# FNet and GeGLU on one core: row moments of h taken by ScalarE, places for gate/up weights four tiles ahead, and the last low half of the hidden DFT weights on VectorE

## The chip, the core and the metric

The kernel runs on one core of one Trainium2 chip. The core has five engines with a queue each: TensorE (PE: matmuls, with weight loads shown as PEld), VectorE (DVE), ScalarE (ACT), GpSimd (POOL) and SyncE (SP), which here issues every DMA transfer. Each engine takes its own instructions in the order in which they were written, and waits for others by semaphores. All DMA goes through one queue of SyncE onto 16 DMA engines. The metric is the device time of one execution in microseconds (us).

## The reference

A pre-LayerNorm FNet mixing layer, followed by a GeGLU feed-forward layer, in float32. S = 2048 tokens, D = 448, DF = 1792.

```python
def _layernorm(x, axis=-1, eps=1e-5):
    m = jnp.mean(x, axis=axis, keepdims=True)
    v = jnp.var(x, axis=axis, keepdims=True)
    return (x - m) / jnp.sqrt(v + eps)
...
a = jnp.einsum("bsd,ed->bse", x, dft_hid_re)
b = jnp.einsum("bsd,ed->bse", x, dft_hid_im)
y = jnp.einsum("ts,bse->bte", dft_seq_re, a) - jnp.einsum("ts,bse->bte", dft_seq_im, b)
...
g = jnp.einsum("bsd,df->bsf", x, w_gate)
u = jnp.einsum("bsd,df->bsf", x, w_up)
h = _gelu(g) * u
return jnp.einsum("bsf,fd->bsd", h, w_down)
...
x = A_x
h = x + _A_ref(_layernorm(x, axis=-1), A_dft_seq_re, A_dft_seq_im, A_dft_hid_re, A_dft_hid_im)
h2 = h + _B_ref(_layernorm(h, axis=-1), B_w_gate, B_w_up, B_w_down)
```

## The kernel before

Every float32 operand of a matmul is split into two float16 parts: ScalarE writes the high half (`hi_part`, line 100) and VectorE the low half (`lo_part`, lines 104 and 106), and a product takes three matmuls. Some products are formed by Strassen's scheme of seven, whose operand sums VectorE or GpSimd form first. All engines' instructions stand in the order in which the program writes them; a table of slots (`slots`, `plan`, with a rank inside a slot) sets that order for the middle of the kernel, and a loop over tiles for its end.

**First tiles (0 to 40 us).** x comes in 16 tiles of 128 tokens. VectorE takes the mean and variance of a row (`x_stats`, BATCH_NORM), ScalarE the root, VectorE the reciprocal with one Newton step (`rstd`, lines 128 to 132) and the normalised tile (line 137). Its halves `xs` are transposed by TensorE for tiles 0 to 3 (`x_turn_pe`, line 374) and by DMA after that, and `feature_mm` (line 412) multiplies them by the hidden DFT weights, which come as four slabs `wh_raw` and are split into `wh_hi` and `wh_lo`. The low half of slab 3 (64 rows) is written by GpSimd in two operations (`wh_low(3, G)`, lines 399 and 400), those of the other slabs by VectorE in one (line 106).

**Sequence DFT (to 362 us).** Eight passes `p` of eight units `u`; each unit loads a block `wr` of DFT weights, splits it into `ws` and runs 48 or 84 matmuls into `acc` (line 508). A place of `wr` is loaded again when its low half has been taken. Into the same slots are woven: the gate/up weights (`Weights`: 14 tiles of 128 columns are loaded as `gu_raw`, summed to `gu_s`, split to `gu_w` and stored as `w_dram`); `seq_out(p)`, in which VectorE adds the bank sums of a pass, over a scratch tile `e`, to x and so makes h in `hx`; and one slot after it the moments of h for the second LayerNorm, `ffn_moments` on VectorE (lines 175 and 176), the root on ScalarE (line 121), `rstd` and, for the first four passes, the normalised operand for the gate/up stage (`xn_h` by ScalarE, its sums and halves, and its transposes by DMA into `hops`). Pass `p` is token pair `(q, j)` with p = 2q + j. The last pair's moments, (3, 1), are taken later, in the tile loop.

**Gate/up and down (362 us to the end).** 56 tiles, `t` = 14 q + f: a quarter `q` of the tokens, against a slab `f` of 128 gate and 128 up columns. `GateUp` does a tile's products into three banks pX, pY and pZ (line 913); in the first quarter a tile is 39 matmuls. The weights of a tile, `gw[t]`, are 0.9 MB read back from `w_dram` (`gw_load`, line 996) into one of three places: two of the pool `ring` and one of `ring3`. Tiles 0, 1 and 2 lie there already, from the split. In iteration t the load of tile t + 2 is issued, and it waits in SyncE's queue until TensorE has last read tile t - 1. The hidden values go into `hh[q]`, two places of a pool `fpool`; `hh[1]` is first written in tile 14. Beside the first quarter the down weights are prepared (`down_prep`): seven loads (line 190), sums by GpSimd (lines 195 to 198), halves by ScalarE and VectorE. From tile 14 on the down products (line 855) run between the gate/up products.

```python
def gw_load(t):
    gw[t] = w_tile(f"gw{t}", ring if t % 3 < 2 else ring3)
    nc.sync.dma_start(gw[t], w_dram[t % NF])
...
if 0 < t < N_GU - 2:
    gw_load(t + 2)
```

Of the kernel before, what the change touches and what calls it, by code (L numbers as in the profile page):

```python
# [32 lines left out]
def kernel(  # L33
# [84 lines left out]
    def root(mv, tag):  # L118
        n = mv.shape[1]
        sd = small.tile([P, n], F32, tag=f"sd{n}", name=f"sd_{tag}")  # L120
        A.activation(sd, mv[:, :, 1], AF.Sqrt, scale=1.0 / X_SC**2, bias=eps_t)
        return sd

    def rstd(mv, sd, tag, pool=small):
# [4 lines left out]
        V.tensor_scalar(r[:, 1], mv[:, :, 1], EPS, -0.5 / X_SC**2, op0=ALU.add, op1=ALU.mult)  # L129
# [40 lines left out]
    def ffn_moments(q, j, h, g):  # L170
# [4 lines left out]
        V.bn_stats(st, h[:, g, :])  # L175
        V.bn_aggr(moments[q, j][:, g, :], st)

    def ffn_root(q, j):
        moments[q, j] = moments[q, j], root(moments[q, j], f"h{q}_{j}")

    def ffn_rstd(q, j):
        mv, sd = moments[q, j]
        moments[q, j] = mv, rstd(mv, sd, f"h{q}_{j}", const)
# [16 lines left out]
    def ffn_norm(q, j, h):  # L200
        tag = f"h{q}_{j}"
        mv, r = moments.pop((q, j))
        xn = fops.tile([P, 2, D], F32, tag="xn", name=f"xn_{tag}")
        for g in range(2):
            normed(xn[:, g, :], h[:, g, :], mv, r, g)
        ffn[q, j] = xn

    def ffn_norm_act(q, j, h):
# [4 lines left out]
        nb = small.tile([P, 2], F32, tag="nb", name=f"nb_{tag}")  # L213
        V.scalar_tensor_tensor(nb, mv[:, :, 0], -1.0, r, op0=ALU.mult, op1=ALU.mult)
# [91 lines left out]

    def x_stats(*tiles):
        n, tag = len(tiles), f"x{tiles[0]}"
        mv = small.tile([P, n, 2], F32, tag=f"mv{n}", name=f"mv_{tag}")
# [4 lines left out]
        norm_x[tiles] = mv  # L314
# [10 lines left out]
    def x_bias(*tiles):  # L325
        mv, r, _ = norm_x[tiles[0]]
        nb = small.tile([P, 2], F32, tag="nb", name=f"nb_x{tiles[0]}")
        V.scalar_tensor_tensor(nb, mv[:, :, 0], -1.0, r, op0=ALU.mult, op1=ALU.mult)
# [7 lines left out]
    def x_norm_v(i):  # L336
# [6 lines left out]
        u, g = divmod(i, 2)  # L343
        if g == 0:
            pool = (fops, p1)[ORDER.index(u) % 2]
            t = pool.tile([P, 2, 2 * D], F16, tag="xs", name=f"xs{u}")
            for k in range(2):
                xs[i + k] = t[:, k, :]
# [179 lines left out]

    def seq_out(p):
        (X, Y, Z, W), _ = acc.pop(p)  # L530
        h = hp[divmod(p, 2)]
        e = fops.tile([P, 4, HD], F32, tag="tt", name=f"e{p}")
# [144 lines left out]
    for p in range(N_PASS):  # L677
# [11 lines left out]
        for g in range(2):  # L689
            plan(n + 1, 5, lambda q=q, j=j, g=g: ffn_moments(q, j, hp[q, j], g))  # L690
# [45 lines left out]
    wh_low(3, G)  # L736
# [15 lines left out]
    x_norm(3)  # L752
    x_lo(3)
# [239 lines left out]

    def gw_load(t):
        gw[t] = w_tile(f"gw{t}", ring if t % 3 < 2 else ring3)
# [173 lines left out]

    cur = GateUp(0)  # L1170
# [6 lines left out]
    for t in range(N_GU):  # L1177
# [5 lines left out]
        if 0 < t < N_GU - 2:  # L1183
            gw_load(t + 2)
# [126 lines left out]
```

## Time and profile before

| | us |
|---|---|
| median of 3 runs (lowest to highest) | 728.72 (728.53 to 728.88) |
| the profiled execution's own time | 728.71 |
| its span, first to last instruction | 726.9 |
| TensorE busy, share of the span | 712.0, 98% |
| mean granted TensorE clock | 0.998 |

How to read the rows below. A row of a timeline has the start (us from the span's first instruction), the time from the first start to the last end, the engine, the line, the operation, what it writes and reads (buffer numbers left out), the shape, how many equal instructions were merged, and in brackets the idle time ahead and what ended it. A row of windows has a stretch, its length, each engine's busy time with its count of instructions (PE, PEld, DVE, ACT, POOL), the granted TensorE clock as a share of full speed (PEclk), the share of the 16 DMA engines that was busy, and GB/s. SPq is SyncE's queue; it issues transfers and is not counted as busy. Where a time is called drawn, it is the matmul's modelled end.

The page's coarse view, 40 equal slices of the span with the busy share of each engine in tenths:

```profile
PE   7999999999999999999999999999999999999998
DVE  6678859998989888989345567576665756667520
ACT  5476644645555545444155555456555545555510
POOL 3023030000000000020014464465563756657230
DMA  8274444897969699685067754757458486555401
```

VectorE is nearly full from slice 7 to slice 18 (110 to 340 us), GpSimd does almost nothing there, and ScalarE stands at about half throughout.

### The profile page before, as it was taken

The page shows a single profiled execution, that of the slowest core. Times are in us where ns is not written, and L with a number is a line of the kernel's source. Part 1 is how long each engine was busy: PE and PEld are TensorE (multiplying, and loading weights), DVE is VectorE, ACT ScalarE, POOL GpSimd, SP SyncE. Part 2 cuts the span into 40 slices and gives each one's busy share as a digit, 9 for nine tenths or more (in the row PEclk, how much of TensorE's full clock was granted, in tenths as well). Part 3 has the DMA queues.
Part 4 walks back from the last instruction along what each step waited for, and adds up shares of the span by engine and source line. Part 5 has one row for each costly group of instructions (what it writes and reads, how often), then busy time and mean ns, then how long its engine had stood idle before and what let it go on. Part 6 is the DMA issues. An engine that isn't in the chain of part 4 may idle for free.

```text
span 726.9 us, 14535 instructions
## 1 busy us (share of the span) xinstructions
PE 712.0 (98%) x5800; PEld 561.6 (77%) x5800; DVE 510.6 (70%) x1043; ACT 365.0 (50%) x748; POOL 207.9 (29%) x237
## 2 busy tenths in 40 slices
PE   7999999999999999999999999999999999999998
PEld 5556566666767666676788789999999999999998
DVE  6678859998989888989345567576665756667520
ACT  5476644645555545444155555456555545555510
POOL 3023030000000000020014464465563756657230
PEclk9999999999999999999999999999999999999999
DMA  8274444897969699685067754757458486555401
GB/s 326 60 187 93 73 171 148 287 256 259 276 240 282 234 275 326 242 298 187 1 223 240 243 191 169 198 179 223 163 171 205 162 215 223 204 200 203 153 15 64
DMA packets 72340, 142.90 MB, mean 197 GB/s; under 512 B 41296, under 2 KB 47568, under 8 KB 72272
## 3 DMA queue, kind: packets, MB, share of 16 engines
q1 hardware_dynamic: 72272, 141.97, 61.1%
q8 instruction: 45, 0.74, 0.4%
q14 instruction: 23, 0.19, 0.1%
HBM read 112.46 MB, written 20.19 MB: 182 GB/s over the span
## 4 chain that ended last, share of the span: by engine, by line
PE 79%; DVE 10%; DMA 5%; ACT 3%; issue 1%; SPq 0%; DVEq 0%; ACTq 0%
PE acc L508 28%; PE pY L913 13%; PE acc_d L855 11%; PE pZ L913 8%; PE pX L913 8%; PE ab L412 7%; DMA gw<-w_dram 3%; DVE ws L106 2%; DVE xs L104 1%; DMA wr<-in_w_seq_dram 1%; PE last_Z L1079 1%; PE last_X L1079 1%; PE last_Y L1079 1%; DMA gu_raw<-in_w_gu_dram 1%; DVE gu_w L106 1%
## 5 line engine op out<-in xcount | busy, mean ns | idle before, releaser
L508 PE MATMUL acc<-b,ws 128*128 128x448 f16 (+1 forms) x1968 | 280.0, 305 | 1.5 <-DVE ws L106 1.5
L508 PEld LDWEIGHTS <-ws 128*128 128x128 f16 x1968 | 190.0, 98 | 91.1 <-DVE ws L106 3.1
L913 PEld LDWEIGHTS <-gw 128*128 128x128 f16 x2067 | 201.4, 98 | 26.9 <-DMA gw<-w_dram 5.4
L913 PE MATMUL pY<-hops,gw 128*128 128x256 f16 x901 | 122.5, 273 | 0.0
L855 PE MATMUL acc_d<-wd,dn_w 128*128 128x224 f16 x882 | 105.1, 259 | 0.0
L855 PEld LDWEIGHTS <-dn_w 128*128 128x128 f16 x882 | 85.0, 98 | 2.8
L106 DVE SCALAR_TENSOR_TENSOR ws<-wr,ws 128x1024 f16<-128x1024 f32 (+2 forms) x88 | 73.7, 859 | 17.6 <-ACT ws L100 16.4
L100 ACT ACTIVATE ws<-wr 128x1024 f16<-128x1024 f32 (+2 forms) x88 | 64.1, 756 | 41.8 <-issue 26.5
L913 PE MATMUL pX<-hops,gw 128*128 128x256 f16 x583 | 79.7, 273 | 4.5 <-DMA gw<-w_dram 4.5
L913 PE MATMUL pZ<-hops,gw 128*128 128x256 f16 x583 | 80.9, 273 | 0.4 <-DVE hh L923 0.3
L195 POOL TENSOR_TENSOR wd_s<-wd 128x448 f32<-128x448 f32 x7 | 8.2, 1170 | 229.1 <-DMA w_dram<-gu_w 209.8
L992 POOL TENSOR_TENSOR hh<-hh,c 128x256 f32<-128x256 f32 x42 | 31.3, 746 | 145.2 <-ACT c L990 145.2
L412 PEld LDWEIGHTS <-xT 128*128 128x128 f16 x352 | 34.7, 99 | 33.0 <-issue 2.6
L104 DVE TENSOR_TENSOR dn_w<-hh,dn_w 128x256 f16<-128x256 f32 x42 | 19.6, 466 | 53.1 <-ACT dn_w L100 53.1
L1010 POOL TENSOR_TENSOR dn_s<-hh 128x256 f32<-128x256 f32 x42 | 52.8, 1256 | 0.0
L104 DVE TENSOR_TENSOR dn_w<-dn_s,dn_w 128x640 f16<-128x640 f32 x42 | 46.2, 1101 | 6.3 <-ACT dn_w L100 5.2
L957 ACT ACTIVATE u<-pY 128x256 f32<-128x256 f32 x56 | 21.4, 382 | 57.3 <-PE pY L913 57.3
L412 PE MATMUL ab<-wh_hi,xT 128*128 128x448 f16 x224 | 46.7, 359 | 0.2
L952 ACT ACTIVATE pY<-pX 128x256 f32<-128x256 f32 x56 | 20.6, 368 | 51.9 <-PE pX L913 51.7
L1009 POOL TENSOR_TENSOR dn_s<-hh 128x256 f32<-128x256 f32 x42 | 37.9, 902 | 0.0
L971 ACT ACTIVATE u<-pY 128x256 f32<-128x256 f32 x56 | 21.4, 382 | 27.2 <-PE pY L913 26.9
L100 ACT ACTIVATE ws<-wsum 128x1024 f16<-128x1024 f32 x24 | 25.2, 1051 | 18.9 <-DVE wsum L472 18.9
(130 smaller groups left out, 899.5 us busy)
## 6 DMA issues: line engine op xcount, KB each, us to landing
gw<-w_dram SPq DMA_DIRECT2D x53, 896.0 KB, 4.7
wr<-in_w_seq_dram SPq DMA_DIRECT2D x64, 512.0 KB, 4.7
w_dram<-gu_w SPq DMA_DIRECT2D x14, 896.0 KB, 7.2
gu_raw<-in_w_gu_dram SPq DMA_DIRECT2D x28, 384.0 KB, 5.6
wd<-in_w_down_dram SPq DMA_DIRECT2D x14, 448.0 KB, 4.3
hx<-in_x_dram SPq DMA_DIRECT2D x8, 448.0 KB, 6.8
h_dram<-hx SPq DMA_DIRECT2D x8, 448.0 KB, 6.8
hr<-h_dram SPq DMA_DIRECT2D x8, 448.0 KB, 5.4
```

What stands on the lines that cost most here:

```text
L100: A.activation(dst, src, AF.Copy, scale=scale)
L104: V.tensor_sub(dst, src, hi)
L106: V.scalar_tensor_tensor(dst, src, scale, hi, op0=ALU.mult, op1=ALU.subtract)
L412: PE.matmul(feat[i][r][:, :D], xT[i][:, kx, :], w[:, kw, r * D : (r + 1) * D], start=n == 0, stop=n == 10,)
L508: PE.matmul(banks[k][:, cols], lhs, rhs, start=k not in begun, stop=stop, skip_group_check=True)
L855: PE.matmul(acc[k // 2][:, k % 2 * HD : (k % 2 + 1) * HD], a_of(la, a), b_of(lb, b), start=first and m == 0 and k % 2 == 0, stop=last and ...
L913: PE.matmul(ps, w[:, wl, wa + ws, :], ops[:, m + ms, :], start=first and n == 0, stop=last and n == len(terms) - 1, skip_group_check=True,)
L957: A.activation(self.u2, self.Y, AF.Copy, scale=SC)
L992: G.tensor_mul(c22, c22, self.c12)
L1009: G.tensor_add(s[:, 0:2], t[:, 0:2], t[:, 2:4])
L1010: G.tensor_sub(s[:, 2:4], t[:, 1:4:2], t[:, 0:4:2])
L1079: PE.matmul(banks[0][:, c * HD : (c + 1) * HD] if one else banks[c][:, 0:HD], last["h"][:, lh, f, tok], w, start=f == 0 and m == 0 and c = ...
```

## The change

Three parts, of which none touches a matmul.

1. The moments of h of the first seven pairs are taken by ScalarE. `act_moments` copies a row and sums it (`accum_out`), scales the sum by -1/D to minus the mean, then squares the row with that as bias and sums again. The copies go to the first half of `e`. So the second moment is D times the variance, and the first is minus the mean: `root`, `rstd` and `bias_of` take a factor `of` (D or 1). The pair (3, 1) keeps VectorE's operations. `ffn_norm`, which nothing called, is gone.
2. Four more places for gate/up weights: a tile `gw_ahead` in the place of `hh[1]`. Tiles 3 to 6 are loaded there ahead of the loop, tiles 10 to 13 again; tiles 7, 8 and 9 go to the three old places, and in iterations 1 to 7 the load of tile t + 6 is issued rather than of t + 2. From tile 14 on all is as before.
3. `wh_low(3)` is done by VectorE in one operation, after `x_norm(3)`.

The allocation of `xs` tiles and the tags of small tiles are written differently, with no effect on the instructions.

```diff
+    def act_moments(mv, src, junk):
+        A.activation(junk, src, AF.Copy, accum_out=mv[:, 0:1])
+        A.activation(mv[:, 0:1], mv[:, 0:1], AF.Copy, scale=-1.0 / D)
+        A.activation(junk, src, AF.Square, bias=mv[:, 0:1], accum_out=mv[:, 1:2])
...
-        A.activation(sd, mv[:, :, 1], AF.Sqrt, scale=1.0 / X_SC**2, bias=eps_t)
+        A.activation(sd, mv[:, :, 1], AF.Sqrt, scale=1.0 / (of * X_SC**2), bias=eps_t)
...
+    def bias_of(nb, mv, r, of=1):
+        V.scalar_tensor_tensor(nb, mv[:, :, 0], 1.0 if of > 1 else -1.0, r, op0=ALU.mult, op1=ALU.mult)
...
+    def moments_of(q, j):
+        return 1 if (q, j) == (NB - 1, 1) else D
+
+    def ffn_moments(q, j, h, g, junk=None):
...
+        if moments_of(q, j) > 1:
+            act_moments(moments[q, j][:, g, :], h[:, g, :], junk)
+            return
...
+    def junk_of(e):
+        return e[:, 0:2].rearrange("p o d -> p (o d)")
...
-            plan(n + 1, 5, lambda q=q, j=j, g=g: ffn_moments(q, j, hp[q, j], g))
+            plan(n + 1, 5, lambda q=q, j=j, g=g: ffn_moments(q, j, hp[q, j], g, junk_of(e_of[2 * q + j])))
...
-    wh_low(3, G)
...
     x_norm(3)
+    wh_low(3)
     x_lo(3)
...
+    ahead = fpool.tile([P, 4, 28 * P], F16, tag="hh", bufs=2, name="gw_ahead")
+
     def gw_load(t):
-        gw[t] = w_tile(f"gw{t}", ring if t % 3 < 2 else ring3)
+        if 3 <= t < 7 or 10 <= t < 14:
+            gw[t] = ahead[:, (t - 3) % 7]
+        else:
+            gw[t] = w_tile(f"gw{t}", ring if t % 3 else ring3)
         nc.sync.dma_start(gw[t], w_dram[t % NF])
...
+    for t in range(3, 7):
+        gw_load(t)
     cur = GateUp(0)
...
-        if 0 < t < N_GU - 2:
+        if 0 < t < 8:
+            gw_load(t + 6)
+        if NF - 2 <= t < N_GU - 2:
             gw_load(t + 2)
```

**Where the instructions stand.** SyncE's queue at the start of the gate/up stage, before (`h_dram7` is the store of the last pass's h, `wd32` the down weights, `gw` the gate/up weights of a tile, `w_dram` where they come from; the last number of a name is a buffer's):

```order
L550 DMA h_dram7_141<-hx7_3518 128x896
L190 DMA wd32_1_4067<-in_w_down_dram 128x896
L996 DMA gw3_4165<-w_dram3_145 128x3584
L996 DMA gw4_4225<-w_dram4_146 128x3584
L190 DMA wd32_2_4283<-in_w_down_dram 128x896
L996 DMA gw5_4289<-w_dram5_147 128x3584
L996 DMA gw6_4349<-w_dram6_148 128x3584
L190 DMA wd32_3_4407<-in_w_down_dram 128x896
L996 DMA gw7_4413<-w_dram7_149 128x3584
L996 DMA gw8_4473<-w_dram8_150 128x3584
L190 DMA wd32_4_4531<-in_w_down_dram 128x896
```

Two loads of gate/up weights stand between each two of the down weights. SyncE's queue at the same place in the change (`gw_ahead` is the new tile of four places):

```order
L564 DMA h_dram7_141<-hx7_3517 128x896
L205 DMA wd32_1_4066<-in_w_down_dram 128x896
L1015 DMA gw_ahead_4084<-w_dram3_145 128x3584
L1015 DMA gw_ahead_4084<-w_dram4_146 128x3584
L1015 DMA gw_ahead_4084<-w_dram5_147 128x3584
L1015 DMA gw_ahead_4084<-w_dram6_148 128x3584
L1015 DMA gw7_4169<-w_dram7_149 128x3584
L1015 DMA gw8_4229<-w_dram8_150 128x3584
L205 DMA wd32_2_4287<-in_w_down_dram 128x896
L1015 DMA gw9_4293<-w_dram9_151 128x3584
L1015 DMA gw_ahead_4084<-w_dram10_152 128x3584
L205 DMA wd32_3_4410<-in_w_down_dram 128x896
```

Six loads of gate/up weights now stand between `wd32_1` and `wd32_2`, where two stood, and the first four of them come ahead of the loop.

ScalarE in the pass that follows the pair (0, 1), before (`gu_w10` and `gu_s10` are a gate/up tile's halves and sums, `ws` the split DFT weights, `sd` the root):

```order
L100 ACTIVATE gu_w10_1774<-gu_raw10_1616 128x512
L100 ACTIVATE gu_w10_1774<-gu_raw10_1616 128x256
L100 ACTIVATE ws2_2_1805<-wr2_2_1614 128x1024
L100 ACTIVATE gu_w10_1774<-gu_s10_1706 128x512 x2
L121 ACTIVATE sd_h0_1_1849<-mv_h0_1_1808,eps_t_79 128x2
L100 ACTIVATE ws2_3_1851<-wr2_3_1670 128x1024
```

The root, which ends the moments, follows the halves of `gu_s10`. ScalarE at the same place in the change (`e1` is the scratch tile, `mv` the two moments):

```order
L100 ACTIVATE gu_w10_1773<-gu_raw10_1615 128x512
L100 ACTIVATE gu_w10_1773<-gu_raw10_1615 128x256
L100 ACTIVATE ws2_2_1804<-wr2_2_1613 128x1024
L120 ACTIVATE e1_1756,mv_h0_1_1807<-hx1_1448 128x448
L121 ACTIVATE mv_h0_1_1807<-mv_h0_1_1807 128x1
L122 ACTIVATE e1_1756,mv_h0_1_1807<-hx1_1448,mv_h0_1_1807 128x448
L120 ACTIVATE e1_1756,mv_h0_1_1807<-hx1_1448 128x448
L121 ACTIVATE mv_h0_1_1807<-mv_h0_1_1807 128x1
L122 ACTIVATE e1_1756,mv_h0_1_1807<-hx1_1448,mv_h0_1_1807 128x448
L100 ACTIVATE gu_w10_1773<-gu_s10_1705 128x512 x2
L127 ACTIVATE sd_h0_1_1848<-mv_h0_1_1807,eps_t_79 128x2
L100 ACTIVATE ws2_3_1850<-wr2_3_1669 128x1024
```

Six instructions for the moments have come in between the split of `wr2_2` and that of `gu_s10`, and the root and the split of `wr2_3` stand behind them. On VectorE the two BN_STATS and two BN_AGGR of that place are gone, here and in the other six pairs.

VectorE in the first tiles, around tile 3 of x (`x_179`), before:

```order
L131 TENSOR_TENSOR r_x_321<-r_x_321 128x1
L132 SCALAR_TENSOR_TENSOR r_x_321<-r_x_321 128x1
L137 TENSOR_SCALAR x_179<-x_179,mv_x_314,r_x_321 128x448
L104 TENSOR_TENSOR xs_279<-x_179,xs_279 128x64
L104 TENSOR_TENSOR xs_279<-x_179,xs_279 128x384
```

The low halves of `xs` follow the normalised tile at once. VectorE at the same place in the change:

```order
L137 TENSOR_TENSOR r_x_319<-r_x_319 128x1
L138 SCALAR_TENSOR_TENSOR r_x_319<-r_x_319 128x1
L146 TENSOR_SCALAR x_179<-x_179,mv_x_312,r_x_319 128x448
L106 SCALAR_TENSOR_TENSOR wh_lo<-wh_raw_170,wh_hi 64x896
L104 TENSOR_TENSOR xs_277<-x_179,xs_277 128x64
L104 TENSOR_TENSOR xs_277<-x_179,xs_277 128x384
```

One row with 64 partitions, the low half of slab 3, has come in ahead of the low halves of `xs`. GpSimd's queue of the same time, before:

```order
L86 MEMSET eps_t 128x1
L381 MEMSET wh_lo 64x896
L399 TENSOR_SCALAR wh_raw_170<-wh_raw_170 64x896
L400 TENSOR_TENSOR wh_lo<-wh_raw_170,wh_hi 64x896
L450 TENSOR_TENSOR b_10_579<-b_10_579 128x448
L451 TENSOR_TENSOR b_10_579<-b_10_579 128x224
```

Rows three and four are the low half of slab 3. GpSimd's queue in the change:

```order
L86 MEMSET eps_t 128x1
L390 MEMSET wh_lo 64x896
L459 TENSOR_TENSOR b_10_578<-b_10_578 128x448
L460 TENSOR_TENSOR b_10_578<-b_10_578 128x224
L461 TENSOR_TENSOR b_10_578<-b_10_578 128x224
```

The two operations on `wh_raw` are gone; the next ones, sums of features for Strassen's scheme, are the same.

More of the change, by code (lines that the diff above doesn't have):

```diff
@@ L212, in ffn_norm_act @@
         xn = fops.tile([P, 2, D], F32, tag="xn", name=f"xn_{tag}")
[L213 to L214 removed]
+        nb = small.tile([P, 2], F32, tag="nb2", name=f"nb_{tag}")
+        bias_of(nb, mv, r, moments_of(q, j))
         for g in range(2):
@@ L326, in x_bias @@
         mv, r, _ = norm_x[tiles[0]]
-        nb = small.tile([P, 2], F32, tag="nb", name=f"nb_x{tiles[0]}")
-        V.scalar_tensor_tensor(nb, mv[:, :, 0], -1.0, r, op0=ALU.mult, op1=ALU.mult)
+        nb = small.tile([P, len(tiles)], F32, tag=f"nb{len(tiles)}", name=f"nb_x{tiles[0]}")
+        bias_of(nb, mv, r)
         for i in tiles:
@@ L342, in x_norm_v @@
             normed(xn, xn, mv, r, g)
[L343 to L348, printed above, removed]
+        xs_tile(i)
     def x_high(i):
```

31 lines of the change are left out of this document (15 added, 16 removed).

## The prediction

> **What bounds the kernel now.** First the page's busy times and the list of who waited for whom (engine, line, what ended the wait: us in total, times, longest).
>
> ```profile
> PE 712.0 (98%) x5800; PEld 561.6 (77%) x5800; DVE 510.6 (70%) x1043; ACT 365.0 (50%) x748; POOL 207.9 (29%) x237
> ```
> ```profile
> PE pX L913 <- DMA gw<-w_dram: 4.5, 3, 1.6
> PE xT_ps L374 <- DVE xs L104: 2.3, 3, 1.9
> PE acc L508 <- DVE ws L106: 1.5, 3, 0.7
> ```
>
> TensorE is the bound: some 15 us of the 726.9 are idle, and the change leaves all of its instructions as they are, so what can be won is idle time. The three waits shown lie in three stages, and the change has one part for each.
>
> **Part 1, weights ahead (4.5 us of idle).** TensorE's rows around the first wait; SyncE's issues; two windows (us; busy time of PE, PEld, DVE, ACT, POOL; PEclk, DMA share, GB/s); GpSimd's and ScalarE's work on the down weights, with the page's time from a load's issue to its landing.
>
> ```profile
> 381.76 0.71 PE L913 MATMUL pX<-hops,gw 128*128 128x256 f16 x5
> 383.81 0.83 PE L913 MATMUL pX<-hops,gw 128*128 128x256 f16 x6 [1.34 <-DMA gw<-w_dram]
> ```
> ```profile
> 365.43 0.32 SPq L550 DMA_DIRECT2D h_dram<-hx  x1
> 365.84 0.38 SPq L190 DMA_DIRECT2D wd<-in_w_down_dram  x1
> 369.22 4.59 SPq L996 DMA_DIRECT2D gw<-w_dram  x2
> 374.47 0.33 SPq L190 DMA_DIRECT2D wd<-in_w_down_dram  x1
> ```
> ```profile
> 366.00:369.00 3.00, 2.92 (x28) 2.46 (x27) 0.78 (x2) 1.87 (x6) 0.00 (x0) 1.00 0.90 292
> 375.00:378.50 3.50, 3.50 (x35) 3.08 (x33) 1.57 (x4) 1.30 (x5) 0.72 (x1) 1.00 0.90 347
> ```
> ```profile
> 389.59 1.13 POOL L195 TENSOR_TENSOR wd_s<-wd 128x448 f32<-128x448 f32 x1 [3.43 <-issue]
> 392.47 1.14 ACT L100 ACTIVATE wd<-wd_s 128x1120 f16<-128x1120 f32 x1 [0.72 <-POOL wd_s L198]
> ...
> 419.98 1.14 ACT L100 ACTIVATE wd<-wd_s 128x1120 f16<-128x1120 f32 x1 [0.91 <-POOL wd_s L198]
> ```
> ```profile
> gw<-w_dram SPq DMA_DIRECT2D x53, 896.0 KB, 4.7
> ```
>
> A row's last matmul is drawn about 0.16 longer than it blocks the next (below, fourteen start at 20.84, last 2.81, and the next row starts at 23.49, after 2.65). So a wait costs 0.16 more than its idle time: 4.5 + 3 x 0.16 = **5.0 us**. They come because gw3 is issued only at 369.22, when tile 0 has freed a place, and each later load is as late.
>
> After the change gw3 to gw6 stand right behind the store and the down weights of 365.43 and 365.84, so they are issued from 366.22 on, 3 us earlier, and wait for no tile. The last columns of the two window rows are the DMA share and GB/s: 347 at a share of 0.90 is 386 GB/s when full. A load of 0.918 MB then takes 2.4 us, at 347 it takes 2.6. The store and down weights keep the engines until about 369 (292 GB/s times 3 us is their 0.9 MB). One alone lands 4.7 after its issue, 2.3 more than it moves; in a queue I put 1 to 2 us of that behind the last byte. So gw3 is in at 372.4 to 373.4, the next three 2.4 apart. A tile of the first quarter is 39 matmuls of 0.109, 4.26 us, and tile 5 was wanted at 381.76 + 5 x 0.109 = 382.3; so tiles 3, 4 and 6 are wanted at 373.8, 378.0 and 386.6, and the loads are in by 373.4, 375.8 and 380.6. Later tiles are requested five tiles ahead. All 5.0 us go.
>
> What is late next: SyncE's queue is in order, and gw7 and gw8 also stand ahead of the second down weights now (issued at 374.47 in both). They come seventh: 369 + 6 x 2.4 + 1.2 = 384.6, landing by 386.6, where GpSimd wants them at 389.59 less the 1.5 us of the first wait, 388.1. The cover is 1.5 us at 386 GB/s and none at 347. If they are late, ScalarE's in-order split of 392.47 and the copies behind it hold TensorE one for one. I take nothing, and keep 0 to 2 us. The place that the four loads take is next written at tile 14, after the last read of gw13: nothing. Renamed tags, views and a later allocation issue nothing: nothing.
>
> **Part 2, the last low half.**
>
> ```profile
> 10.71 1.08 DVE L106 SCALAR_TENSOR_TENSOR wh_lo<-wh_raw,wh_hi 128x896 f16<-128x896 f32 x1
> ...
> 13.70 0.66 DVE L137 TENSOR_SCALAR x<-x,mv_x,r_x 128x448 f32<-128x448 f32 x1
> 14.28 2.75 DVE L106 SCALAR_TENSOR_TENSOR wh_lo<-wh_raw,wh_hi 128x896 f16<-128x896 f32 x1
> ...
> 20.06 0.51 DVE L137 TENSOR_SCALAR x<-x,mv_x,r_x 128x448 f32<-128x448 f32 x1
> 21.21 0.69 DVE L104 TENSOR_TENSOR xs<-x,xs 128x64 f16<-128x64 f32 x2 [0.64 <-ACT xs L100]
> ```
> ```profile
> 11.00 3.11 POOL L399 TENSOR_SCALAR wh_raw<-wh_raw 64x896 f32<-64x896 f32 x1 [8.75 <-ACT wh_hi L100]
> 14.19 1.89 POOL L400 TENSOR_TENSOR wh_lo<-wh_raw,wh_hi 64x896 f16<-64x896 f32 x1
> ```
> ```profile
> 15.02 0.34 PE L374 MATMUL xT_ps<-ident,xs 128*128 128x128 f16 x3 [1.12 <-ACT xs L100]
> 17.23 0.27 PE L374 MATMUL xT_ps<-ident,xs 128*128 128x128 f16 x1 [1.86 <-DVE xs L104]
> ...
> 17.99 2.45 PE L412 MATMUL ab<-wh_hi,xT 128*128 128x448 f16 x6
> 20.23 0.77 PE L412 MATMUL ab<-wh_lo,xT 128*128 128x448 f16 x2
> 20.84 2.81 PE L412 MATMUL ab<-wh_hi,xT 128*128 128x448 f16 x14
> 23.49 0.55 PE L374 MATMUL xT_ps<-ident,xs 128*128 128x128 f16 x7
> ```
> ```profile
> 13.90:17.25 3.35, 0.37 (x5) 0.20 (x4) 3.35 (x4) 0.58 (x1) 2.10 (x2) 1.00 1.06 386
> 17.35:20.65 3.30, 3.10 (x12) 1.41 (x12) 3.08 (x10) 1.32 (x4) 0.00 (x0) 0.50 0.20 76
> 20.75:24.00 3.25, 3.25 (x24) 1.86 (x22) 2.11 (x6) 0.52 (x2) 0.00 (x0) 1.00 0.00 0
> ```
>
> The same VectorE operation takes 1.08 and, beside GpSimd's of 14.19 to 16.08, 2.75: it ends about 1 us after GpSimd does. The operation at 13.70 takes 0.66 where its twin at 20.06, with GpSimd idle, takes 0.51. With GpSimd gone: 1.67 + 0.15 = **1.8 us**, and TensorE waits for just this (17.23). VectorE's new operation has the same columns, about 1.06, and stands ahead of 21.21, where VectorE idles 0.64; its net 0.4 is covered, since the product of it is wanted by the transposes of 23.49, 1.5 us later.
>
> There is a second loss behind it. PEclk, third column from the right, is 0.50 in 17.35:20.65: the eight matmuls from 17.99 take 2.85 us, where the fourteen from 20.84 take 2.65, 0.189 each. That is 2.85 - 8 x 0.189 = **1.3 us**. The stretch ahead of it had TensorE busy for 0.37 of 3.35 us. There its two waits, 1.12 and 1.86 and their tails, make 3.3 us; the 1.8 leave 1.5 of them. The bounds are 0 (the clock halves all the same) and 1.3; no row has a stretch half busy, so the nearest row that kept its clock (20.75:24.00, wholly busy) and the one that lost it lie far on both sides. I take 1.3, because no stretch of that length is nearly idle any more.
>
> The Trainium skill ("TensorE: Matmul & The Clock Gate", Part 1: The HAM clock gate) says that the clock halves after an idle window of about 3.4 us on a free-running grid and returns after a busy one; the half-speed stretch here, bounded by 17.25 and 20.75, agrees. By that rule the 1.3 us are won; if a window half idle counted too, they are not.
>
> With both, the transposes of 23.49 come at 20.3 and VectorE's halves for them at about 20.1 to 20.5: level, so I give 0.1 back.
>
> **Part 3, moments by ScalarE.** VectorE's and ScalarE's rows of one pass, and two ScalarE rows for prices.
>
> ```profile
> 156.72 1.15 DVE L545 TENSOR_TENSOR hx<-hx,e 128x448 f32<-128x448 f32 x2
> ...
> 161.94 0.62 DVE L175 BATCH_NORM_STATS2 st_h<-hx 128x6 f32<-128x448 f32 x1
> ...
> 163.41 1.26 DVE L106 SCALAR_TENSOR_TENSOR gu_w<-gu_s,gu_w 128x512 f16<-128x512 f32 x2
> ```
> ```profile
> 156.44 1.06 ACT L100 ACTIVATE ws<-wr 128x1024 f16<-128x1024 f32 x1 [1.88 <-issue]
> 157.41 1.13 ACT L100 ACTIVATE gu_w<-gu_s 128x512 f16<-128x512 f32 x2
> 163.53 0.29 ACT L121 ACTIVATE sd_h<-mv_h,eps_t 128x2 f32<-128x2 f32 x1 [4.99 <-DVE mv_h L176]
> ```
> ```profile
> 9.51 0.56 ACT L100 ACTIVATE xs<-x 128x448 f16<-128x448 f32 x1
> ...
> 27.64 0.76 ACT L340 ACTIVATE x<-x,nb_x,r_x 128x448 f32<-128x448 f32 x1 [1.64 <-DVE nb_x L328]
> ```
>
> VectorE is rid of 163.41 - 161.94 = 1.47 us in each of seven passes. TensorE loses 1.5 + 3 x 0.16 = 2.0 us to it in three of them, 0.5 to 0.8 each, less than 1.47. So **2.0 us** go if ScalarE does not hand the delay back. Its new work per pass is two times a copy (0.56), a small scale (0.29) and a square with a pointer (0.76): 3.2 us. The write of the sums shows in no row: below, 2.4 (overlaps of a tenth, cheaper ends); above, another 0.29 for each of four sums, 4.4. I take 3.2, made of the nearest rows. Queued behind it are the split of 157.41, for which VectorE now comes at 161.94, and the root. From 157.5 to 161.94, less 0.6 for the first half, are 3.8 us, and VectorE's spare 0.9 (1.47 less 0.58) makes 4.7: both ends fit. ScalarE's idle 4.99 hides it; the other four passes lose nothing now.
>
> ScalarE takes more time than VectorE saves. The Trainium skill ("ScalarE: Activation LUTs", Rules for kernel authors) puts add, mul and the like on VectorE rather than ScalarE; 3.2 against 1.47 agrees with its preference, yet here VectorE is the engine waited for. Keeping to that rule would leave the 2.0 us where they are.
>
> **The sum.** The profiled execution is 728.71 with a span of 726.9 (the 1.8 outside stay); the median is 728.72. 5.0 + 1.8 + 1.3 + 2.0 - 0.1 = 10.0. Another 0.1 for the third wait of part 1: ScalarE's split of 419.98 waits 0.19 longer than that of 392.47, and the wait hid it. 728.7 - 9.9 = **718.8 us**.
>
> **The rivals.**
> - The clock halves all the same: 718.8 + 1.3 = 720.1. For it, 1.5 us stay idle; against it, no stretch is as idle as that with 0.37.
> - Second down weights late: up to 2 us, 719.3 to 720.8. For it, seven transfers in a row; against, 386 GB/s.
> - The sums cost ScalarE 5.4 us a pass, 0.7 over what fits: the 2.0 stay, 720.8.
> - The change does not do what it says, the four loads landing no earlier: 723.8. The issue at 366.22 speaks against it.
> - Slower: the strict order of ScalarE. From 4.7 us on, every us goes to TensorE in the three passes bound by VectorE. To use up the 9.9 it takes 3.3 more in each, 8.0 us of moments, 2.5 times my price; at 9 us the time is 728.7 + 3 x 1.0 = 731.7. Nothing but the unseen price of a sum speaks for it.
>
> **How the numbers follow.** Forecast 0.46; clock 0.23; down weights 0.11; dearer sums 0.10; loads no earlier, or two rivals at once, 0.06; slower 0.04. Range 717.8 (1 us of other short waits gone as well) to 722.0 (clock and one more rival): it leaves out some 0.1 above and little below. 0.2% is 1.5 us, about what a measurement can tell: faster 0.94, same 0.02, slower 0.04.
>
> **What would show it.** Waits of pX for gw gone, and gw3 landing by 373.4; VectorE's wh_lo at some 14.1 with 1.1 us, and PEclk 1.00 up to 24 us; the six ScalarE rows taking 2.4 to 4.4 a pass, and no wait of acc for ws. A wait of ScalarE or GpSimd for the down weights near 386, PEclk of 0.5, or ScalarE rows of 2 us each would prove me wrong.

## The result and the profile after

| | before | after |
|---|---|---|
| median of 4 executions each (us) | 728.80 | 718.68 |
| lowest to highest | 728.53 to 733.30 | 718.21 to 720.39 |
| profiled execution | 728.71 | 718.65 |
| its span, mean granted clock | 726.9, 0.998 | 716.9, 1.0 |

The ratio is 0.985, 95% interval 0.981 to 0.989: the change makes the kernel about 10.1 us faster, and 718.8 was forecast. The page's busy times, then the list of TensorE's waits:

```profile
PE 709.5 (99%) x5800; PEld 562.2 (78%) x5800; DVE 500.0 (70%) x1016; ACT 386.1 (54%) x818; POOL 203.2 (28%) x235
```
```profile
PE xT_ps L383 <- ACT xs L100: 1.0, 1, 1.0
PE xT_ps L383 <- DVE xs L104: 0.4, 2, 0.2
...
PE ab L421 <- DVE b L106: 0.2, 1, 0.2
PE acc L517 <- DVE ws L106: 0.2, 1, 0.2
```

The waits of pX for gw (4.5) are gone, those of acc for ws fell from 1.5 to 0.2, those of xT_ps for VectorE's xs from 2.3 to 0.4. VectorE is rid of 10.6 us: seven passes of 1.47 are 10.3, and the low halves of the hidden DFT weights take 4.3 us in four operations where they took 4.9 in three. ScalarE has 21.1 more.

The first tiles, by windows and by VectorE's rows. The stretches are those shown of before:

```profile
13.90:17.25 3.35, 2.00 (x14) 1.13 (x15) 3.31 (x7) 1.87 (x4) 0.00 (x0) 1.00 1.05 383
17.35:20.65 3.30, 3.30 (x24) 1.93 (x23) 3.19 (x11) 0.65 (x2) 0.00 (x0) 1.00 0.22 85
```
```profile
13.64 0.51 DVE L146 TENSOR_SCALAR x<-x,mv_x,r_x 128x448 f32<-128x448 f32 x1
14.07 1.08 DVE L106 SCALAR_TENSOR_TENSOR wh_lo<-wh_raw,wh_hi 128x896 f16<-128x896 f32 x1
```

VectorE's low half takes 1.08 where it took 2.75, the normalisation 0.51 where it took 0.66. TensorE is busy for 2.00 of the first stretch (0.37 before), and PEclk in the second is 1.00 (0.50 before).

ScalarE's moments in one pass, and VectorE's split that waits for what stands behind them:

```profile
154.59 0.56 ACT L120 ACTIVATE e<-hx 128x448 f32<-128x448 f32 x1
155.06 0.19 ACT L120 ACTIVATION_READ_ACCUMULATOR e<-hx 128x1 f32 x1
155.28 0.20 ACT L121 ACTIVATE mv_h<-mv_h 128x1 f32<-128x1 f32 x1
155.51 0.67 ACT L122 ACTIVATE e<-hx,mv_h 128x448 f32<-128x448 f32 x1
156.09 0.19 ACT L122 ACTIVATION_READ_ACCUMULATOR e<-hx,mv_h 128x1 f32 x1
...
157.91 1.13 ACT L100 ACTIVATE gu_w<-gu_s 128x512 f16<-128x512 f32 x2
```
```profile
158.99 1.29 DVE L106 SCALAR_TENSOR_TENSOR gu_w<-gu_s,gu_w 128x512 f16<-128x512 f32 x2
```

Each sum is an instruction of its own, of 0.19, behind the one that sums. From 154.59 to the next work's start at 157.91 are 3.3 us; 3.2 were forecast. The first of the two halves in the split's row is ready about 157.91 + 0.57 = 158.5, and VectorE takes it at 158.99 without idling.

SyncE's four early loads are issued from 361.28 on, and the first lands at 367.34. GpSimd's first use of the second down weights, and two of the windows in which the loads move (DMA share and GB/s last):

```profile
383.04 1.13 POOL L210 TENSOR_TENSOR wd_s<-wd 128x448 f32<-128x448 f32 x1 [2.87 <-DVE wd L106]
```
```profile
367.00:370.00 3.00, 3.00 (x30) 2.70 (x28) 1.38 (x3) 2.60 (x6) 0.00 (x0) 1.00 1.01 423
...
382.00:385.00 3.00, 3.00 (x30) 2.69 (x29) 1.50 (x3) 1.89 (x6) 1.96 (x2) 1.00 1.02 411
```

GpSimd waits for VectorE there, not for the transfer: the second down weights landed at 380.85, 2.2 us ahead of their use.

### The profile page after: what moved, and what is told of

Same layout as the page of the kernel before. It is cut to its first block, busy times and chain, and to the rows that moved or that the text cites. A ratio compares the mean times of both kernels' runs of the same rounds, so it can differ in the third digit from the quotient of the medians.

```text
span 716.9 us, 14587 instructions
## 1 busy us (share of the span) xinstructions
PE 709.5 (99%) x5800; PEld 562.2 (78%) x5800; DVE 500.0 (70%) x1016; ACT 386.1 (54%) x818; POOL 203.2 (28%) x235
## 4 chain that ended last, share of the span: by engine, by line
PE 83%; DVE 8%; ACT 5%; DMA 2%; issue 1%; SPq 0%; ACTq 0%; DVEq 0%
PE acc L517 36%; PE pY L927 14%; PE acc_d L869 11%; PE pZ L927 9%; PE pX L927 9%; ACT b L100 1%; DVE xs L104 1%; PE last_Z L1098 1%; PE last_X L1098 1%; PE last_Y L1098 1%; DVE st_x L327 1%; ACT x L354 1%; ACT xs L100 1%; DMA w_dram<-gu_w 1%; DMA wh_raw<-in_w_hid_dram 1%
## 5 line engine op out<-in xcount | busy, mean ns | idle before, releaser
L927 PEld LDWEIGHTS <-gw 128*128 128x128 f16 x1755 | 171.5, 98 | 17.7 <-issue 0.8
L927 PE MATMUL pY<-hops,gw 128*128 128x256 f16 x765 | 105.2, 273 | 0.0
L927 PE MATMUL pZ<-hops,gw 128*128 128x256 f16 x495 | 68.7, 273 | 0.4 <-DVE hh L937 0.3
L927 PE MATMUL pX<-hops,gw 128*128 128x256 f16 x495 | 68.4, 273 | 0.0
L860 POOL TENSOR_TENSOR hr<-hr,v 128x224 f32<-128x224 f32 x48 | 33.4, 717 | 0.1
```

The source lines that it names most:

```text
L860: op(x, x, m)
L927: PE.matmul(ps, w[:, wl, wa + ws, :], ops[:, m + ms, :], start=first and n == 0, stop=last and n == len(terms) - 1, skip_group_check=True,)
```

## The experiments

The changed kernel ran ten times in two groups, 718.17 to 720.39 with a median of 718.8, and "over the changed kernel" below means that. The kernel before ran beside each group: medians 730.72, 730.00 and 729.56 us on three chips (11, 23 and 28 executions, 725.11 to 734.04). Its spread is a finding of its own, taken up under the clock.

### The three parts, undone one at a time

**e1_no_ahead: part 1 undone.**

```diff
-    ahead = fpool.tile([P, 4, 28 * P], F16, tag="hh", bufs=2, name="gw_ahead")
...
-    for t in range(3, 7):
-        gw_load(t)
...
-        if 0 < t < 8:
-            gw_load(t + 6)
-        if NF - 2 <= t < N_GU - 2:
+        if 0 < t < N_GU - 2:
             gw_load(t + 2)
```

> The changed kernel with part 1 taken out: the gate/up loads stand where they stood before the change, each issued when a tile has freed its place; parts 2 and 3 stay. Theory (the three waits of pX for gw are worth 5.0 us and nothing else replaces them): 718.7 + 5.0 = 723.7 us, with the three waits of 4.5 us in sum back in the list of waits, and no other stage changed. Rival (the second down weights, which the change asks for behind nine loads, cost the changed kernel something, so part 1 is worth less than its waits): 720 to 722.5, and a wait of the changed kernel behind 383 us that is gone here.

Measured: 722.45 us (721.31 to 724.17, 6 executions, all at clock 1.0), 3.7 over the changed kernel. TensorE's rows with a wait, 365 to 415 us:

```profile
379.80 0.83 PE L927 MATMUL pX<-hops,gw 128*128 128x256 f16 x6 [1.75 <-DMA gw<-w_dram]
388.93 0.83 PE L927 MATMUL pX<-hops,gw 128*128 128x256 f16 x6 [0.43 <-DMA gw<-w_dram]
407.61 0.83 PE L927 MATMUL pX<-hops,gw 128*128 128x256 f16 x6 [1.48 <-DMA gw<-w_dram]
```

The same three waits are back. Their size is not fixed: most loads landed 4.4 to 4.7 us after their issue, those waited for 6.5, 5.2 and 6.2, and a tile takes 4.26. The profiled execution took 723.52, near the theory's 723.7, but not by the waits of pX alone: they are 3.7 us in sum where 4.5 were expected, and its waits of xT_ps for VectorE's xs in the first tiles, which the edit does not touch, are 1.1 us where the changed kernel's profile has 0.4. The median is 1.3 under the theory, and the executions spread over 2.9 us where those of e8_order, below, which has part 1 and ran on the same chip, spread over 0.4. The median lies just inside the rival's range (720 to 722.5). The rival's cause, a wait of the changed kernel behind 383 us that is gone here, has nothing to show: that kernel has no such wait.

**e2_low_pool: part 2 undone.**

```diff
+    wh_low(3, G)
     x_stats(2)
...
     x_norm(3)
-    wh_low(3)
     x_lo(3)
```

> The changed kernel with the last low half of the Fourier weights back on GpSimd, at its old place; parts 1 and 3 stay. Theory (1.8 us of VectorE's slowing, and behind it 1.3 us of half clock): 718.7 + 3.1 = 721.8 us, VectorE's second wh_lo operation back at 2.7 us where it is 1.08, and PEclk 0.50 in the stretch behind 17.3 us. Rival (the clock is a matter of where its window falls, not of the idle time alone): the 1.8 us return alone, 720.5, with PEclk 1.00 there in most executions.

Measured: 721.82 (721.55 to 723.03, 5 executions), 3.0 over the changed kernel. The mean clock was 0.998 in three and 0.995 in two, in none 1.0. VectorE's rows and two windows:

```profile
13.52 0.66 DVE L146 TENSOR_SCALAR x<-x,mv_x,r_x 128x448 f32<-128x448 f32 x1
14.10 2.75 DVE L106 SCALAR_TENSOR_TENSOR wh_lo<-wh_raw,wh_hi 128x896 f16<-128x896 f32 x1
```
```profile
13.70:17.10 3.40, 0.42 (x5) 0.23 (x4) 3.40 (x4) 0.58 (x1) 2.12 (x2) 1.00 1.05 385
17.20:20.50 3.30, 3.06 (x12) 1.43 (x12) 3.05 (x10) 1.35 (x4) 0.00 (x0) 0.54 0.27 101
```

Both losses return, the slowing and the half clock behind it, at the forecast price in sum. The rival is out: no execution kept the clock.

**e3_dve_moments: part 3 undone.**

```diff
     def moments_of(q, j):
-        return 1 if (q, j) == (NB - 1, 1) else D
+        return 1
```

> The changed kernel with the moments of h on VectorE again in all passes; parts 1 and 2 stay. Theory (TensorE waits for VectorE's ws in three of the passes, 0.5 to 0.8 us each): 718.7 + 2.0 = 720.7 us, with the three waits of acc for ws back, 1.5 us in sum. Rival 1 (ScalarE's strict order hands the delay back, so that part 3 is worth nothing): 718.7. Rival 2 (VectorE's 1.47 us a pass count in full): 718.7 + 3 x 1.47 = 723.1.

Measured: 721.02 (720.54 to 721.72, 5 executions), 2.2 over the changed kernel.

```profile
PE acc L517 <- DVE ws L106: 1.8, 5, 0.7
```

The waits are back, five of them in three passes. Both rivals, 718.7 and 723.1, are out.

### What the first tiles still lose

**e8_order: TensorE's order.**

```diff
     x_lo(2)
+    feature_mm(1, range(4, 8))
     x_turn_pe(2, 0, 4)
     x_turn_pe(2, 4, 7)
-    feature_mm(1, range(4, 8))
```

> The changed kernel with one more edit in the first tiles: the second half of tile 1's Fourier products stands ahead of tile 2's transposes in TensorE's order, so that TensorE has work while it would wait for tile 2's halves. Theory (the three waits of xT_ps between 14.8 and 16.0 us, 1.4 us in sum, are what TensorE still loses there, and those products need nothing that is late): 1.2 to 1.5 us less, 717.2 to 717.5. Rival (the products need the low half that VectorE finishes at 15.15, so the wait only changes its name): 718.7, with a wait of ab for wh_lo in its place.

Measured: 718.72 (718.51 to 718.87, 5 executions): no change. The time is the rival's, but the reason is neither's: no wait of ab for wh_lo has come in. The products did fill the wait ahead of tile 2's transposes (0.23 us is left there), but three waits of 0.27, 0.18 and 0.24 us stand ahead of tile 3's, at 19.14 to 20.12 us, where the changed kernel has none. VectorE, which makes the low halves, starts those of tile 3 at 19.39, against 19.61 in the changed kernel. TensorE's order was not the limit.

**e9_order2: VectorE's order too.**

```diff
-    wh_low(2)
     x_rstd(3)
     x_norm(3)
-    wh_low(3)
     x_lo(3)
+    wh_low(2)
+    wh_low(3)
```

> The reordered kernel (e8_order) with VectorE's order changed too: the two last low halves behind tile 3's normalisation and halves, not ahead of them. In e8_order the three waits only moved to tile 3's transposes (19.14 to 20.12 us, 1.2 us lost), which wait for halves that stand behind two low halves of 1.06 each on VectorE. Theory (VectorE's order is what TensorE waits for): these waits go, 718.7 - 1.1 = 717.6 us. Rival (the low halves are then late for tile 0's last products): 718.2 to 718.7, with a wait of ab for wh_lo near 20 us.

Measured: 720.43 (719.99 to 721.19, 6 executions), 1.6 slower than the changed kernel. TensorE's rows:

```profile
20.39 0.34 PE L383 MATMUL xT_ps<-ident,xs 128*128 128x128 f16 x3 [0.24 <-DVE xs L104]
20.57 0.54 PE L421 MATMUL ab<-wh_lo,xT 128*128 128x448 f16 x2
21.39 0.54 PE L421 MATMUL ab<-wh_lo,xT 128*128 128x448 f16 x2 [0.28 <-DVE wh_lo L106]
22.39 3.20 PE L421 MATMUL ab<-wh_lo,xT 128*128 128x448 f16 x16 [0.46 <-DVE wh_lo L106]
```

The rival had the wait right: the two low halves are late for tile 0's last products. It had the time wrong, by some 1.7 us. In the profiled execution 1.0 of that is another thing: the second tile of x landed at 6.99 us (5.28 in the changed kernel's profile), and VectorE idled 1.08 us for it. Whether it was late in the other five is not on record, so the size of what the order costs stays open. No version tried beat the changed kernel.

### The clock

**after_again: the changed kernel once more.** No edit.

> The changed kernel itself, unchanged, to see how often its clock falls by half in the first tiles. Theory (the clock halves when a stretch of some 3.4 us at fixed places on the time axis falls on TensorE's waits there; about 1.35 of 3.35 us are still idle): most executions at 718.2 to 718.8 with a mean clock of 1.0, one in four at 720.4 with 0.998, as in its first four. Rival (that one execution was noise of another kind): all within 0.4 us of 718.6, clock 1.0 in all.

Measured: 719.04 (718.17 to 719.46, 6 executions), the clock 1.0 in all six. So the 720.39 of the first four, at 0.998, was one execution in ten, not one in four. Neither case was right in full: the clock is the rival's, but at that clock the times still spread over 1.3 us, not within 0.4 of 718.6.

**e5_filler and e12_filler45: the kernel before, with 20 and with 45 transposes more in TensorE's wait.** The low half stays on GpSimd.

```diff
     feature_mm(1, range(4))
+    pw2 = ps_dft.tile([P, 8, P], F16, tag="A", name="pw2")
+    for k in range(20):    # 45 in e12_filler45
+        PE.transpose(pw2[:, k % 8, :], ident, ident)
     wh_low(1)
```

> The kernel before the change, with twenty transposes more that nobody reads, put on TensorE ahead of tile 2's transposes, where it waits for VectorE: they keep TensorE busy in the wait without shortening it. Theory (idle time ahead is what halves the clock): VectorE's low half still takes 2.75 and tile 2's transposes still wait for it to the same moment, but PEclk is 1.00 from 17.3 us on and each execution is 1.3 us shorter than one of the kernel before with one halved stretch (728.7), so 727.4, with a mean clock of 1.0. Rival (the half clock has another cause, or comes from an earlier stretch): 728.7, clock 0.998.

> As e5_filler, with 45 transposes in place of 20: in e5_filler the stretch with the filler (17.1 to 20.5 us of its profile) was still busy for only 1.79 of 3.40 and the next one ran at half clock. 45 of 0.056 are 2.5 us, which leaves some 0.8 idle. Theory (a stretch that is idle for about half of it still halves the clock, one that is mostly busy does not): no half clock between 17 and 24 us in the profile, executions at a mean clock of 0.998 or more except those that lost it earlier, and a median 1 to 1.5 us under that of e5_filler against the same kernel before, so near 727. Rival (the filler does not count as work, or the wait itself is the cause): clock and time as in e5_filler, 728.0 and 0.998.

Measured: e5_filler 728.00 us (12 executions, ratio to the kernel before beside it 0.9971 [0.9948, 0.9993]), clock 0.995 in three, 0.998 in five, 0.999 in one, 1.0 in three. e12_filler45 727.23 us (12, 0.9966 [0.9945, 0.9986]), clock 1.0 in ten, 0.999 and 0.998 in one each. Windows of e5_filler, in steps of 3.4 us:

```profile
6.90:10.30 3.40, 1.89 (x13) 0.92 (x14) 2.80 (x11) 1.96 (x4) 0.00 (x0) 0.99 1.02 388
10.30:13.70 3.40, 3.40 (x16) 1.81 (x15) 2.64 (x6) 1.81 (x4) 1.64 (x1) 0.51 1.04 410
13.70:17.10 3.40, 3.40 (x34) 2.21 (x31) 2.28 (x5) 1.02 (x3) 3.32 (x2) 1.00 1.05 388
17.10:20.50 3.40, 1.79 (x14) 0.94 (x13) 3.33 (x8) 1.86 (x4) 0.03 (x1) 0.99 0.24 88
20.50:23.90 3.40, 3.40 (x11) 1.40 (x10) 2.65 (x10) 0.58 (x1) 0.00 (x0) 0.51 0.00 0
```

And of e12_filler45:

```profile
13.70:17.10 3.40, 3.02 (x50) 2.75 (x48) 3.36 (x3) 0.58 (x1) 2.44 (x2) 1.00 1.06 388
17.10:20.50 3.40, 2.89 (x18) 1.57 (x19) 3.26 (x12) 1.29 (x3) 0.00 (x0) 1.00 0.28 107
20.50:23.90 3.40, 3.40 (x25) 1.94 (x24) 2.33 (x7) 1.87 (x5) 0.00 (x0) 1.00 0.00 0
```

In e5_filler two stretches that are drawn busy for 1.89 and 1.79 of 3.40 are each followed by one at half clock. With 20 transposes the clock still fell, in eight of twelve executions, so the forecast of e5_filler missed. In e12_filler45 VectorE's low half still takes 2.77 and tile 2's transposes still wait for it, but the stretches ahead are busy for 2.9 and more, and the clock stays. So TensorE's idle time is the cause: work that nobody reads keeps the clock, though the wait ends no earlier.

How much idle time it takes is not told by the busy share alone. The clock of e5_filler falls at 10.20 and 20.44 us and returns at 13.62 and 23.86, so it changes at points that lie 3.41 us or a multiple of it apart. Further stretches between such points, one later in e5_filler and one in the kernel before, are drawn busy for as little, and the clock stays. First e5_filler, then the kernel before:

```profile
412.97:416.38 3.41, 1.80 (x17) 1.62 (x18) 1.09 (x1) 2.27 (x5) 0.78 (x2) 1.00 0.90 287
416.38:419.80 3.42, 3.42 (x34) 3.07 (x32) 2.08 (x5) 1.03 (x4) 1.92 (x3) 1.00 0.51 146
```
```profile
399.57:402.98 3.41, 1.81 (x18) 1.39 (x16) 1.96 (x3) 2.10 (x4) 2.06 (x3) 1.00 0.69 232
402.98:406.39 3.41, 3.41 (x34) 3.06 (x32) 0.83 (x2) 1.45 (x4) 0.72 (x1) 1.00 0.77 305
```

The drawn time overstates the work where rows are short and many, as in the first tiles, since each row's last matmul is drawn past the start of the next. Counted instead at the pace of back-to-back matmuls (0.189 us for 448 columns, 0.109 for 256, 0.056 for 128), an estimate from TensorE's rows in each stretch, the two stretches that cost the clock hold 1.3 us of work each, and the two that did not hold 1.8 and 1.6. The border lies somewhere between; no run was made to find it.

The forecast of the time was rougher: 727.23 is the number that was expected of e12_filler45, but it was to be 1 to 1.5 us under e5_filler against the kernel before beside each, and the two ratios do not differ. Against its own kernel before, e12_filler45 is 2.3 us faster (1.0 to 4.0), about what the half clock costs there. e5_filler's first half-clock stretch has a cause that no expectation held: VectorE idles 1.42 us at 7.36 for the second tile of x, which landed late. That is a matter of the execution; in the profile of the kernel before it was on time.

The 62 further executions of the kernel before, by mean clock: 5 at 1.0 (median 727.68), 18 at 0.998 (728.70), 4 at 0.997, 29 at 0.995 (731.06), 6 at 0.993 (733.40). One stretch of 3.4 us at half clock takes 0.5 x 3.4 / 727 = 0.0023 off the mean, so these are none, one, two and three stretches. The clock is not all of the spread: the executions at 0.995 alone lie between 727.60 and 733.65. The execution in which the prediction was made had one.

**e10_part2_alone: the kernel before with part 2 alone.**

```diff
-    wh_low(3, G)
...
     x_norm(3)
+    wh_low(3)
     x_lo(3)
```

> The kernel before with part 2 alone: the last low half on VectorE ahead of tile 3's halves. Theory (part 2 is worth 1.8 us of slowing and the half clock, which on the chips of these runs costs the kernel before one to three stretches of 1.3 to 1.6 us): 3.1 us or more under the kernel before beside it, mean clock 1.0, waits of pX for gw and of acc for ws unchanged; about 725.6. Rival (the parts need one another): less than 1.8 us.

Measured: 726.84 (722.94 to 730.52, 12 executions), ratio 0.9963 [0.9936, 0.9990], 2.7 us under the kernel before beside it; clock 1.0 in nine, 0.998 in three.

```profile
PE pX L913 <- DMA gw<-w_dram: 4.5, 3, 2.0
PE acc L508 <- DVE ws L106: 2.3, 5, 0.7
```

Part 2 works alone: the clock is at 1.0 in nine of twelve, where the kernel before beside it has 3 of 28. The time is less sure. 2.7 us falls short of the 3.1 or more that were expected, and the interval, 0.7 to 4.7 us, holds the rival's figure too. The waits of the other parts stay. The nine executions at clock 1.0 still spread from 722.94 to 727.72, where the six of after_again, which have part 1, spread over 1.3.

### The room behind ScalarE and behind the loads

**e6_moments_twice and e11_moments_half: more time for the moments.** The moments of e6_moments_twice are all done twice; in e11_moments_half those of one half of each pair.

```diff
         if moments_of(q, j) > 1:
-            act_moments(moments[q, j][:, g, :], h[:, g, :], junk)
+            for _ in range(2):    # 1 + g in e11_moments_half
+                act_moments(moments[q, j][:, g, :], h[:, g, :], junk)
             return
```

> The changed kernel with each of ScalarE's moment sequences done twice, the second time with the same result, so that they take 6.8 us a pass instead of 3.4. Theory of the prediction (ScalarE has room for 4.7 us in the three passes where VectorE was waited for, and from there each us goes to TensorE through its strict order): (6.8 - 4.7) x 3 = 6.3 more, 725.0 us, with waits of acc for ws in those passes. Rival (ScalarE's idle time takes it, since it is half idle on the page): 718.7. A third case, the other four passes having no room either: up to 7 x 2.1 = 14.7 more, 733.4.

> The changed kernel with ScalarE's moments done twice for one of the two halves of each tile pair, the second time with the same result: 5.1 us a pass in place of 3.4. Doubled throughout, 6.8 us, they cost 10.5 us in four passes instead of the 6.3 in three that the prediction's bound of 4.7 gives. Theory A (the bound of 4.7 holds in the three passes and the fourth pass bends later): 3 x 0.4 = 1.2 us, 720.0. Theory B (the line through 3.4 and 6.8 without a bound): half of the loss, 5.2 us, 724.0. Theory C (ScalarE has room beyond 5.1): 718.8.

Measured: e6_moments_twice 729.20 us (728.45 to 730.12, 12 executions), 10.4 over the changed kernel; e11_moments_half 722.62 (722.23 to 723.30, 6), 3.8 over. The first lies between the prediction's 725.0 and the third case's 733.4; of the second, none of the three theories (720.0, 724.0, 718.8) holds. VectorE's rows in e11_moments_half, with ScalarE's moments at 155.75 to 160.92:

```profile
159.12 1.22 DVE L106 SCALAR_TENSOR_TENSOR ws<-wr,ws 128x1024 f16<-128x1024 f32 x1
161.47 1.29 DVE L106 SCALAR_TENSOR_TENSOR gu_w<-gu_s,gu_w 128x512 f16<-128x512 f32 x2 [1.12 <-ACT gu_w L100]
163.12 1.23 DVE L106 SCALAR_TENSOR_TENSOR ws<-wr,ws 128x1024 f16<-128x1024 f32 x1 [0.36 <-ACT ws L100]
```

VectorE idles 1.12 + 0.36 = 1.5 us behind the moments, as ScalarE's strict order has it. What TensorE loses is counted from its rows, start to start of two matmuls less what back-to-back ones of the shape take (0.189 for 448 columns, half of it for 224). In two of the passes (217 and 253 us) it loses 0.8 us each, in the first of the three (175 to 182 us) 2.0. That is more than VectorE idled in the rows shown, because its delay had begun a pass earlier. Matched instruction by instruction with the changed kernel, VectorE falls back by 1.7 us behind the moments at 124 to 129 us, where TensorE loses only 0.1; it makes up none of it, falls back by another 1.7 behind those shown, and then TensorE falls back by 2.1. At 6.8 us of moments TensorE loses 3.6 in that pass, 2.3 in each of the two, and 1.8 in a fourth, the one from 146 to 161.

**e7_delay: two transfers more ahead of the second down weights.**

```diff
     for t in range(3, 7):
         gw_load(t)
+    for k in range(2):
+        spare = dram.tile([P, 28 * P], F16, name=f"spare{k}")
+        nc.sync.dma_start(spare, w_dram[7 + k])
```

> The changed kernel with two transfers more of 0.9 MB each (copies of weights to a place that nobody reads) in SyncE's queue behind the four early loads, ahead of gw7, gw8 and the second down weights. In the changed kernel these weights landed at 380.85 and GpSimd took them at 383.04, 2.2 us later. Theory (the cover of the second down weights is 2.2 us, and beyond it TensorE is held one for one): two copies at the pace of the loads (2.2 each) bring the landing to 385.2 and cost 2.2 us, 720.9, with GpSimd waiting for wd near 385; if a copy takes twice the time of a load the landing is 389.6 and the cost up to 6.6, 725.3. Rival (there is more room behind GpSimd than that): 718.7 in spite of a late landing.

Measured: 723.66 (721.17 to 725.59, 9 executions); 721.69 is the median of the three at clock 1.0, 2.9 over the changed kernel. The second down weights landed at 385.60. TensorE's row with a wait, GpSimd's, and two windows:

```profile
390.74 1.44 PE L927 MATMUL pY<-hops,gw 128*128 128x256 f16 x6 [2.72 <-ACT pY L966]
```
```profile
385.76 1.13 POOL L210 TENSOR_TENSOR wd_s<-wd 128x448 f32<-128x448 f32 x1 [5.44 <-DMA wd<-in_w_down_dram]
```
```profile
387.00:390.50 3.50, 1.02 (x10) 0.76 (x8) 0.37 (x1) 1.49 (x3) 2.66 (x3) 1.00 1.02 408
390.50:394.00 3.50, 3.26 (x16) 2.33 (x16) 0.85 (x2) 1.17 (x4) 0.72 (x1) 0.52 1.01 415
```

GpSimd starts 385.76 - 383.04 = 2.72 us later than in the changed kernel, and TensorE waits 2.72: one for one, as the theory has it; its price of 2.2 us was 0.5 short. In the profiled execution the wait also halves the clock behind it, as the last window shows. Six of the nine executions have a mean clock of 0.998 or 0.995, which no case had priced, and this puts the median between the theory's two figures, 720.9 and 725.3.

## Why the prediction was right, point by point

- **Part 1, 5.0 us: right.** All three waits went. The loads moved faster than worked out, at 411 to 423 GB/s and 2.2 us apart, not 386 and 2.4; so the cover of the second down weights was 2.2 us, not 1.5, and that rival stayed away. e7_delay shows that it was a real one, and dearer than priced. What the step did not see is that the 4.5 us of waits are one draw. It put them down to gw3's late issue, with each later load as late; but in the profile of the kernel before the three gate/up loads that TensorE waited for took 6.1 to 6.3 us to land, and those between them 4.4 to 4.8. Undone, the part costs 3.7 in the median.
- **Part 2, 1.8 + 1.3 us: right in sum; on the clock by a smaller margin than the prediction knew.** e2_low_pool gives 3.0, e10_part2_alone 2.7 in reverse (0.7 to 4.7). The two terms were not timed apart in the changed kernel, but e12_filler45 shows that the idle time ahead is what halves the clock. The reason given for taking 1.3, that no stretch is nearly idle any more, was not enough: e5_filler's two stretches were not nearly idle either, and they cost the clock. Nor was it so that no row had a stretch half busy; the kernel before has the one at 399.57, busy for 1.81 of 3.41, with the clock kept behind it. In the trace of the changed kernel the clock records put one stretch at 13.83 to 17.25, nearly the window shown above. Counted as under e5_filler it holds 1.6 us of work, where 1.3 cost the clock. That it stayed above is in part luck. The rival "the clock halves all the same" had a chance of 0.23; one of ten executions has a mean clock of 0.998, and where it fell there no trace shows. The Trainium skill ("TensorE: Matmul & The Clock Gate", Part 1: The HAM clock gate) has a free-running grid of about 3.4 us; the trace agrees with it, since e5_filler's clock changes at 10.20, 13.62, 20.44 and 23.86 us. The table that the Trainium skill gives there speaks of an idle window; the trace does not agree if that means a window without work, since two with 1.3 us of matmuls counted as well.
- **Part 3, 2.0 us: right**, 2.2 when undone. The price of 3.2 was 3.3. The sums are four instructions of 0.19, against the bound of 0.29 each, and the scale was cheaper (0.20 for 0.29).
- **The room for the moments: wrong.** "Both ends fit" up to 4.7 us was worked out for one pass by itself. The 3.8 of it that lie ahead of VectorE's split hold: with 3.3 us of moments the split has 0.5 in hand, with 5.2 VectorE idles. The 0.9 of spare behind that is not there anew in each pass. It was read in the pass whose wait comes at 184 us in the kernel before; with longer moments just that pass loses the most (at 175 to 182 us in e11_moments_half), because VectorE brings the delay of the pass before along. The passes in which TensorE loses nothing are not free either, since they hand their delay on. So the slower rival's turning point of 8.0 us was too far: at 6.8 the kernel is at 729.2, its time before, and the whole gain is gone. The measured 3.3 lay inside, so the time was not touched.
- **The small terms: about right in size, wrong in place.** 0.1 was given back at tile 3's transposes and 0.1 at the third wait of part 1; the profile has no wait at either. TensorE loses some 0.3 at 37 us instead:

```profile
37.38 0.35 PE L421 MATMUL ab<-wh_hi,xT 128*128 128x448 f16 x1
37.91 1.29 PE L421 MATMUL ab<-wh_hi,xT 128*128 128x448 f16 x6 [0.18 <-DVE b L106]
```

The row at 37.38 is one matmul that is alone for 0.53 where back-to-back ones start 0.19 apart. TensorE, 3 us earlier, catches up with VectorE there; with part 2 undone (e2_low_pool) 0.2 is lost at that place, so 0.1 is given back. Another 0.2 is given back at 101 us, where the one wait of acc for ws that is left costs 0.33 (0.12 in the kernel before).

One thing stays open. The parts undone singly are worth 3.7 + 3.0 + 2.2 = 8.9 us. The kernel before was 10.1 over the changed one in the first executions and 10.8 to 11.9 in the later groups. Part of that is the clock, which fell two or three times in 35 of the 62 later executions; how the difference divides between the loads, late tiles of x and the clock was not separated.

## What to carry to other kernels

A wait of a few us on TensorE costs its own length and, when it leaves little work between two points at which the clock can change, a stretch at half clock behind it; so remove or fill the longest waits first, and price both. Where work is moved to a half-idle engine with strict order, the room is the time until the next instruction in its queue is wanted, and it must be followed from pass to pass, since an engine that is nearly full brings the delay of one pass into the next. A transfer that takes 4.5 us most times and 6 at others must be asked for more than one tile ahead: the waits that it causes are no fixed sum.

## What the runs showed of the hardware

- TensorE's clock changes at points a multiple of 3.41 us apart, and halves behind a stretch with too little work, not only behind an empty one: 1.3 us of matmuls between two points were too little (e5_filler, twice, busy as drawn for 1.8 to 1.9), 1.6 were enough (the kernel before at 399.57, the changed kernel at 13.83).
- Transposes count as work for it: with 45 of them in the wait (e12_filler45) the mean clock is 1.0 in ten of twelve executions, against 5 of 62 without.
- A row's sum by ScalarE (`accum_out`) is a second instruction of 0.19 us in ScalarE's queue.
- VectorE's one-input normalisation took 0.66 for 0.51 beside GpSimd's one-input operation. Its two-input low half took 2.75 for 1.08 beside GpSimd's two-input one and ended some 1 us after it. e2_low_pool shows both again.
- Loads from DRAM on SyncE's queue ran at 411 to 423 GB/s on one core over 18 us (367 to 385 us of the changed kernel).
